# Loading the keys of one head pair and the values of the pair before it as one row of 56,832 B per partition, in a two-layer decode step

## The chip, the cores and the metric

The kernel runs on one core of one Trainium2 chip. The metric is the device time of one execution in microseconds (us); the time before is the median of three runs, 517.92 us (517.42 to 518.12).

## The reference, cut to what matters

One token (`Sq = 1`, width 640) passes twice through the same attention layer and the same MLP, with the same weights and the same cache both times. There are 32 heads of width 192, each with its own keys and values, and attention sees the last 4,096 positions.

```python
W = min(4096, max(256, Sk // 4))
q = (x @ wq)                                  # 640 -> 32 heads x 192
scores = einsum("bhqd,bhkd->bhqk", q, k) * Dh ** -0.5
o = einsum("bhqk,bhkd->bhqd", softmax(scores), v)
attention = o @ wo
mlp = (sigmoid(x @ w_gate) * (x @ w_up)) @ w_down
x = x + attention(layernorm(x)); x = x + mlp(layernorm(x))      # twice
```

## The kernel before, in words

**Units.** The 32 heads are handled as 16 pairs (`NPAIR`). A pair has two units of 14,208 bf16 values, 28,416 B, in each of the 128 partitions. The unit "a" holds the query weights of the pair and its keys; it lies in DRAM as `ua[p]`. The unit "b" holds its values (12,288 elements, `VE`) and its rows of the output weights (1,920 elements, `WOE`); it lies as `ub[p]`. One DMA loads one unit: 128 rows, one for each partition.

**Places.** One SBUF tensor, `big`, holds seven slots of one unit each and a region of 12,288 elements behind them (line 120), in which the MLP's weights and, in layer 1, the values of pair 1 (`PM`) are put. `big` is laid at a 256 B boundary, after the tensors `cst` and `sh`; `cst` is allocated first, at the default alignment of 32 B. `A_SLOT` and `B_SLOT` (lines 184 to 190) say which slot a unit goes to: in layer 0 the keys alternate between slots 0 and 1, the values between 2 and 3. Pairs 0, 14 and 15 stay in SBUF for layer 1 (`KEPT`), as does the key unit of pair 1, so that layer 1 begins with them while the stream goes on.

**Order of the loads.** `seq` (lines 195 to 209) is the one list of loads, issued in that order by SP: keys 0, keys 1, values 0, output weights of pair 0 into slot 2 (`wo0`), keys 2, values 1, and so on; the last values of each layer come in parts (`b1`, `b0`); then the MLP's weights, and for layer 1 the same from pair 2 to pair 13. `prefetch` (line 288) issues the next load as soon as the program, written down in the order of the compute, has released its slot (`release`): a key unit after the scores of its pair (QK, line 369), a value unit after the product with the output weights (PVn, line 454). On the chip SP waits at each load for a semaphore that says so. Each slot has one semaphore for its loads (`s0` to `s6`), and each user of a slot waits for that slot's load.

**One step** (lines 467 to 478) of pair p: PVn of pair p-2 (in layer 0), the query (Q, line 351), the scores (QK, line 366), the maximum over them (lines 376 to 385) by DVE, ACT and a matmul (line 382), the exponential (line 390), the product of values p-1 (PVmm, line 420), the transposition of the exponentials (ET, line 396), the normalized output of pair p-1 (PVt, line 436), and in layer 1 PVn of pair p-1 (line 450). PE takes its instructions in this order. The steps of pairs 2 to 15 in layer 0 and 4 to 13 in layer 1 are loops on PE; a loop needs the same addresses in each second step, which is why the output weights of pair 0 are in slot 2 in layer 0, and POOL copies them to slot 5, behind the values of pair 0, for layer 1 (line 460).

**The end.** After the last values come the gate, up and down weights of the last MLP (`fg`, `fu`, `fd`); between the loops and the last product (line 634), GpSimd (POOL) clears the semaphores and all engines meet (lines 759 and 760).

Of the kernel before, what the change touches and what calls it, by code (L numbers as in the profile page):

```python
# [13 lines left out]
P = 128  # L14
# [91 lines left out]
def decode_kernel(ctx: ExitStack, nc, cx: bass.AP, ua: bass.AP, ub: bass.AP,  # L106
# [10 lines left out]

    cst = sb("cst", [P, CE + CE % 2], BF16)
    sh = sb("sh", [P, 6 * DC + 8 + FC], BF16, 4)
    big = sb("big", [P, NSLOT * UNIT + ME], BF16, 256)  # L120
    M0 = NSLOT * UNIT
# [5 lines left out]
    sc = sb("sc", [P, 24 + 5 * DC + 2 * FC], FP32)  # L127
# [7 lines left out]
    ones_f = ones_c.to_broadcast([P, P])  # L135
    xq = sh[:, 0:DC]
# [29 lines left out]
    rslot = [res(f"slot{i}") for i in range(NSLOT)]  # L166
    rc = [res(f"cell{i}") for i in range(-(-ME // FW))]
# [4 lines left out]

    def slot(s, o, n):
        return big[:, s * UNIT + o:s * UNIT + o + n]
# [9 lines left out]
    A_SLOT = [{p: p % 2 for p in range(NPAIR)}, {p: 5 if p % 2 else 2 for p in range(NPAIR)}]  # L184
    B_SLOT = [{p: 2 + p % 2 for p in range(NPAIR)}, {p: 3 if p % 2 else 6 for p in range(NPAIR)}]
# [9 lines left out]
    def stream(l, ps):  # L195
        q = list(ps)
        out_ = []
        for i, p in enumerate(q):
            out_.append(("a", l, p))
            if i:  # L200
                out_.append(("b", l, q[i - 1]))
        return out_ + [("b1", l, q[-1]), ("b0", l, q[-1], 0), ("b0", l, q[-1], 1)]
    seq = stream(0, range(NPAIR))
    seq.insert(seq.index(("b", 0, 0)) + 1, ("wo0",))
    seq += [("wol", 14), ("wol", 15)] + [(k,) for k in (*MW, *MV)]
    tail = stream(1, range(2, 14))
    assert tail[0] == ("a", 1, 2)
    seq += [("wom",), ("a0", 0), ("a0", 1)] + tail[1:]
    seq += [("fg",), ("fu",), ("fd", 0), ("fd", 1), ("fd", 2)]
    seq_pos = [0]  # L210
    busy = {2}
# [12 lines left out]

    def try_load(it):
        k = it[0]
        if k in ("a", "b"):
            s = (A_SLOT if k == "a" else B_SLOT)[it[1]][it[2]]
            if not take(s):
                return False  # L230
            n, n0 = VE if it in (("b", 0, 0), ("b", 0, 14)) else UNIT, len(pg.ops["dma"])
            pg.dma(q_dma(slot(s, 0, n), (ua if k == "a" else ub)[it[2]][:, 0:n]), f"s{s}", wr=[rslot[s]])
            if it == ("b", 0, 14):
                ev_done["b14"] = list(pg.ops["dma"][n0]["deps"].items())
        elif k == "b1":
            s = B_SLOT[it[1]][it[2]]
            if not take(s):
                return False
            n, o1 = len(pg.ops["dma"]), UNIT if it[1] else VE
            pg.dma(q_dma(slot(s, NB * DH, o1 - NB * DH), ub[it[2]][:, NB * DH:o1]), f"s{s}", wr=[rslot[s]])  # L240
            ev_done["b1"] = list(pg.ops["dma"][n]["deps"].items())
        elif k == "b0":
            s = B_SLOT[it[1]][it[2]]
            o = it[3] * NHALF
            pg.dma(q_dma(slot(s, o, NHALF), ub[it[2]][:, o:o + NHALF]), f"bh{it[3]}", wr=[res(f"bh{it[3]}")], extra=ev_done["b1"])
        elif k == "a0":
            if f"a14_{it[1]}" not in ev_done:
                return False
            s = A_SLOT[1][2]
            o0, o1 = ((0, A0CUT), (A0CUT, UNIT))[it[1]]  # L250
            pg.dma(q_dma(slot(s, o0, o1 - o0), ua[2][:, o0:o1]), f"a0{it[1]}", wr=[res(f"a0{it[1]}")] + ([rslot[s]] if it[1] else []),
                   extra=[ev_done[f"a14_{it[1]}"]])
        elif k == "wo0":
            s = B_SLOT[0][2]
            pg.dma(q_dma(slot(s, VE, WOE), ub[0][:, VE:UNIT]), f"s{s}", wr=[rslot[s]])
        elif k == "wol":
            s = B_SLOT[0][it[1]]
            pg.dma(q_dma(slot(s, VE, WOE), ub[it[1]][:, VE:UNIT]), f"wol{it[1]}", wr=[res(f"wol{it[1]}")], extra=ev_done["b1" if it[1] == 15 else "b14"])
        elif k in MW:
            if any(n not in ev_done for n in MAFTER.get(k, ())):  # L260
                return False
            c, f0, f1 = MW[k]
            src = {"w": wg_d, "u": wu_d, "d": wd_d}[k[0]]
            pg.dma(q_dma(mreg(c * FW, (f1 - f0) * FW), src[:, f0 * FW:f1 * FW]), k, wr=rc[c:c + f1 - f0])
        elif k in MV:
            if VAFTER[k] not in ev_done:
                return False
            c0, c1 = MV[k]
            o0, o1 = c0 * FW, min(c1 * FW, ME)
            pg.dma(q_dma(mreg(o0, o1 - o0), ub[PM][:, o0:o1]), k, wr=rc[c0:c1])  # L270
        elif k == "wom":
            if "QM" not in ev_done:
                return False
            pg.dma(q_dma(slot(A_SLOT[1][PM], 0, WOE), ub[PM][:, VE:UNIT]), "wom", wr=[res("wom")], extra=[ev_done["QM"]])
        elif k == "fg":
            pg.dma(q_dma(mreg(0, 12 * FW), wg_d), "fg", wr=rc)
        elif k == "fu":
            if not take(U_SLOT):
                return False
            pg.dma(q_dma(slot(U_SLOT, 0, 12 * FW), wu_d), f"s{U_SLOT}", wr=[rslot[U_SLOT]])  # L280
        else:
            if it[1] == 0 and not take(D_SLOT):
                return False
            c0, c1 = WFIN[it[1]]
            pg.dma(q_dma(slot(D_SLOT, c0 * D, (c1 - c0) * D), wdp(c0, c1)), f"wf{it[1]}", wr=[rslot[D_SLOT]] if it[1] == 0 else [])
        return True
# [13 lines left out]
    pg.dma(q_dma(cst[:, 0:CE], cx), "x", wr=[res("cst")], q="adma")  # L300
    prefetch()
# [35 lines left out]
    def attention(l, xi):  # L337
# [70 lines left out]
        def PVmm(p, z):  # L408
# [3 lines left out]
            for h in (1, 0) if half else (0, 1):  # L412
                vt = (mreg(h * NB * DH, NB * DH) if inm else slot(sv, h * NB * DH, NB * DH)).rearrange("p (t d) -> p t d", t=NB)
                for part in (0, 1) if half and h == 0 else (None,):
                    us = range(NB // 2) if part is None else range(part * NB // 4, (part + 1) * NB // 4)

                    def f(t, h=h, vt=vt, us=us):
                        for u in us:
                            j = u % 4
                            ins = t.matmul(o8[h][32 * j:32 * j + 2, 0:2 * DH].rearrange("p (a d) -> p a d", a=2), lhsT=et_sb[:, z, h * NB + 2 * u:h * NB + 2 * u + 2],  # L420
                                           rhs=vt[:, 2 * u:2 * u + 2, :], start=(u < 4), stop=(u >= NB // 2 - 4), tile_position=(0, 32 * j))
                        return ins
                    rV = rc if inm else [rslot[sv]] + ([] if part is None else [res(f"bh{part}")])
                    pg.op("pe", f, rd=[res(f"et{z}")] + rV, ex=[rb[4 + h]])
                pg.op("act", lambda a, h=h: a.copy(out=o8_sb[:, :, h * DH:(h + 1) * DH], in_=o8[h][:, 0:2 * DH].rearrange("p (a d) -> p a d", a=2)),  # L425
                      wr=[res(f"o8sb{h}")], ex=[rb[4 + h]])
# [15 lines left out]
        def PVn(p, z):  # L442
            inm = l == 1 and p == PM
            sv = None if inm else 2 if l == 0 and p == 0 else B_SLOT[l][p]
            wo = slot(A_SLOT[1][PM], 0, WOE) if inm else slot(sv, VE, WOE)
# [8 lines left out]
            pg.op("pe", im, rd=[res(f"oTb{z}")] + ([res("wom"), rslot[sa]] if inm else [rslot[sv]]) + ([res(f"wol{p}")] if p > 13 or (l == 1 and p == 0) else []), ex=[rb[7]])  # L454
            if inm:
                release(sa)
            elif not (l == 0 and ("b", p) in KEPT):
                release(sv)
            if l == 0 and p == 0:
                pg.op("pool", lambda g: g.tensor_copy(out=slot(5, VE, WOE), in_=slot(2, VE, WOE)), rd=[rslot[2]], wr=[res("wol0")])  # L460
                release(2)
# [302 lines left out]
def _layout(inputs):  # L764
# [6 lines left out]
    ua = np.empty((NPAIR, P, UNIT), bf)  # L771
    ub = np.empty((NPAIR, P, UNIT), bf)
    q = wq.reshape(DC, P, NPAIR, 2, DH)
    qv = ua[:, :, :WQE].reshape(NPAIR, P, DC, 2 * DH)
    for h in range(2):
        qv[..., h * P:(h + 1) * P] = q[:, :, :, h, :P].transpose(2, 1, 0, 3)
        qv[..., 2 * P + h * 64:2 * P + (h + 1) * 64] = q[:, :, :, h, P:].transpose(2, 1, 0, 3)
        ua[:, :, WQE + h * W:WQE + (h + 1) * W] = k[:, h, :, :P].transpose(0, 2, 1)
        ua[:, h * 64:(h + 1) * 64, WQE + 2 * W:] = k[:, h, :, P:].transpose(0, 2, 1)
    ua[:, :, :WQE] = qv.reshape(NPAIR, P, WQE)  # L780
    ub[:, :, :VE] = v.transpose(0, 5, 1, 2, 4, 3, 6).reshape(NPAIR, P, VE)
    ub[:, :, VE:] = wo.reshape(NPAIR, P, WOE)
# [19 lines left out]
    return dict(cx=cx, ua=ua, ub=ub, wg=blk(wg), wu=blk(wu), wd=wdn)  # L802
# [17 lines left out]
```

## Time and profile before

| | |
|---|---|
| median of three runs | 517.92 us |
| the profiled execution's own time | 518.12 us |
| its span | 516.8 us |
| PE, DVE, ACT, POOL busy | 275.3, 97.9, 87.7, 2.0 us |
| moved by DMA | 219.45 MB, 11,835 packets |
| transfers of 3,552 KB (one unit): keys, values | 27, 24 |
| from issue to landing, median: keys, values | 29.8, 28.2 us |
| mean granted TensorE clock | 0.598 |

The span is the time from the first to the last instruction or packet; the run's time has 1.3 us more around it. Busy times are shares of engines that work at the same time, so they do not add up. The time from issue to landing has in it the time that a transfer stands in the queue behind earlier ones. In the timeline, times are us from the span's start; the column after the start is the length, and what stands in brackets is how long the engine had been idle and what ended that.

### The profile page before, as it was taken

The numbers are of one execution on the slowest core, as the hardware profiler recorded it, in microseconds if no ns is written. First come the engines' busy times: TensorE is split into PE (matmuls) and PEld (weight loads), VectorE is DVE, ScalarE is ACT, GpSimd is POOL, SyncE is SP. The second block draws the span as 40 slices with busy tenths as digits, with TensorE's granted clock in tenths as the row PEclk, the third lists the DMA queues.
The fourth block names the chain that finished last, engine by engine and source line by source line (L and its number), as shares of the span: only waits on it lengthen the run. The fifth ranks groups of instructions, "written<-read, shape, count | busy, mean of one in ns | idle before, by whom it ended". The sixth has DMA issues, their size and how long they took to land.

```text
span 516.8 us, 8422 instructions
## 1 busy us (share of the span) xinstructions
PE 275.3 (53%) x3716; PEld 139.7 (27%) x3716; DVE 97.9 (19%) x372; ACT 87.7 (17%) x171; POOL 2.0 (0%) x5
## 2 busy tenths in 40 slices
PE   0645454544545453635465667777554545455465
PEld 0322122212222222212224434433222212222234
DVE  1222111211121201111121233232211211121211
ACT  0112102210121112210120023123202211121120
POOL 0010000000000000000000000000000000000000
PEclk9987566556555555565565568666566555555555
DMA  8999999999999999999999999999999999999996
GB/s 357 430 436 432 427 435 433 427 435 440 427 433 438 431 427 438 433 429 431 433 417 411 392 440 428 430 437 432 430 433 432 427 435 433 431 436 435 423 427 282
DMA packets 11835, 219.45 MB, mean 425 GB/s; under 512 B 1448, under 2 KB 1448, under 8 KB 4264
## 3 DMA queue, kind: packets, MB, share of 16 engines
q1 hardware_dynamic: 11672, 219.13, 99.1%
q8 instruction: 13, 0.21, 0.1%
q10 hardware_dynamic: 144, 0.06, 0.0%
q14 instruction: 6, 0.05, 0.0%
HBM read 219.18 MB, written 0.00 MB: 424 GB/s over the span
## 4 chain that ended last, share of the span: by engine, by line
DMA 73%; PE 18%; DVE 4%; SPq 2%; issue 1%; ACT 1%; ACTq 0%; DVEq 0%
DMA big<-in_ub_dram 61%; PE o L420 8%; DMA big<-in_wd_dram 7%; DMA big<-in_wu_dram 4%; PE scores L366 3%; PE bank L403 2%; SPq L182 2%; PE bank L450 1%; PE bank L396 1%; ACT e_sb L390 1%; DVE sc L405 1%; PE bank L382 1%; DVE et_sb L400 1%; DVE sh L439 1%; PE bank L351 1%
## 5 line engine op out<-in xcount | busy, mean ns | idle before, releaser
L420 PE MATMUL o<-big,et_sb 128*2 128x384 bf16 x1024 | 85.7, 508 | 50.1 <-DMA big<-in_ub_dram 50.0
L366 PE MATMUL scores<-big,qs 128*32 128x512 bf16 x744 | 83.0, 614 | 9.9 <-DVE qs L354 9.8
L379 ACT ACTIVATE diag<-cst,sc 128x128 f32<-128x128 bf16 x32 | 12.9, 402 | 262.5 <-DVE sc L376 247.7
L351 PE MATMUL bank<-sh,big 128*128 128x1 bf16 x480 | 17.6, 166 | 69.3 <-DMA big<-in_ua_dram 68.3
L420 PEld LDWEIGHTS o<-big,et_sb 128*2 128x2 bf16 x1024 | 29.0, 113 | 93.7 <-DMA big<-in_ub_dram 58.9
L376 DVE TENSOR_REDUCE sc<-scores 128x1 f32<-128x1024 f32 x31 | 37.9, 1224 | 80.9 <-PE scores L366 80.9
L382 PE MATMUL bank<-diag,sc 128*128 128x128 f32 x64 | 23.1, 458 | 47.4 <-ACT diag L379 47.4
L390 ACT ACTIVATE e_sb<-scores,sc 128x1024 bf16<-128x1024 f32 x31 | 37.3, 1204 | 41.5 <-DVE sc L385 39.7
L425 ACT CAST o_sb<-o 128x384 bf16<-128x384 f32 x64 | 30.4, 476 | 71.3 <-PE o L420 71.2
L366 PEld LDWEIGHTS scores<-big,qs 128*32 128x32 bf16 x744 | 23.7, 132 | 44.3 <-issue 31.1
L351 PEld LDWEIGHTS bank<-sh,big 128*128 128x128 bf16 x480 | 15.8, 106 | 72.2 <-DMA big<-in_ua_dram 70.1
L382 PEld LDWEIGHTS bank<-diag,sc 128*128 128x128 f32 x64 | 14.5, 282 | 72.6 <-ACT diag L379 70.8
L400 DVE CAST et_sb<-bank 128x64 bf16<-128x64 f32 x32 | 7.2, 224 | 122.9 <-PE bank L396 122.9
L354 DVE TENSOR_TENSOR qs<-bank,cst 128x96 bf16<-128x96 f32 x32 | 8.2, 258 | 100.5 <-PE bank L351 100.3
L450 PE MATMUL bank<-sh,big 128*128 128x1 bf16 x480 | 17.4, 165 | 15.5 <-DVE sh L439 15.3
L403 PE MATMUL bank<-sc 128*128 128x2 f32 x64 | 16.0, 319 | 14.5 <-DVE sc L401 14.5
L450 PEld LDWEIGHTS bank<-sh,big 128*128 128x128 bf16 x480 | 14.8, 101 | 18.0 <-DVE sh L439 17.3
L403 PEld LDWEIGHTS bank<-sc 128*128 128x128 f32 x64 | 13.2, 257 | 17.3 <-DVE sc L401 17.3
L383 DVE TENSOR_REDUCE sc<-bank 128x2 f32<-128x128 f32 x32 | 9.3, 292 | 42.5 <-PE bank L382 42.5
L396 PEld LDWEIGHTS bank<-cst,e_sb 128*128 128x128 bf16 x256 | 9.2, 104 | 23.3 <-ACT o_sb L425 16.8
L396 PE MATMUL bank<-cst,e_sb 128*128 128x8 bf16 x256 | 11.9, 170 | 5.7 <-ACT e_sb L390 5.7
L405 DVE RECIPROCAL sc<-bank 64x1 f32<-64x1 f32 x64 | 10.6, 166 | 20.0 <-PE bank L403 18.9
(61 smaller groups left out, 100.6 us busy)
## 6 DMA issues: line engine op xcount, KB each, us to landing
big<-in_ua_dram SPq DMA_DIRECT2D x27, 3552.0 KB, 29.8
big<-in_ub_dram SPq DMA_DIRECT2D x24, 3552.0 KB, 28.2
big<-in_ub_dram SPq DMA_DIRECT2D x2, 3072.0 KB, 26.6
big<-in_ub_dram SPq DMA_DIRECT2D x4, 768.0 KB, 17.2
big<-in_wd_dram SPq DMA_DIRECT2D x3, 960.0 KB, 7.1
big<-in_ua_dram SPq DMA_DIRECT2D x1, 2048.0 KB, 12.2
big<-in_ub_dram SPq DMA_DIRECT2D x1, 2016.0 KB, 16.2
big<-in_ub_dram SPq DMA_DIRECT2D x4, 480.0 KB, 17.8
```

What stands on the lines that cost most here:

```text
L351: ins = t.matmul(qe[:, i:i + 1], lhsT=slot(sa, c * 2 * DH + c0, P), rhs=xq[:, c:c + 1], start=(c == 0), stop=(c == DC - 1))
L366: ins = t.matmul(sc_x[1 + b][32 * j:32 * j + 32, :], lhsT=qs[:, y, k, :], rhs=slot(sa, WQE + k * W + (4 * b + j) * 512, 512), start=(k == ...
L376: pg.op("dve", lambda v: v.reduce_max(out=mx, in_=sc_x[0][:], axis=AX.X), wr=[res("mx")], ex=sc_x[3:5])
L379: pg.op("act", lambda a: a.mul(out=diag[:], in_=ident, mul=mx), rd=[res("cst"), res("mx")], wr=[res("diag")])
L382: pg.op("pe", lambda t: t.matmul(dmx[:, 0:P], lhsT=ones_f, rhs=diag[:], start=True, stop=True), rd=[res("diag"), res("ones")], ex=[rb[2]])
L390: pg.op("act", lambda a: a.activation(out=e_sb[:], in_=sc_x[0][:], func=ACT.Exp, bias=nbias, scale=srs_c, accum_out=rowsum), rd=[res("nbia ...
L396: ins = t.matmul(qe[:, 0:2 * NB].rearrange("p (r x) -> p r x", r=2)[:, :, 4 * b:4 * b + 4], lhsT=e_sb[:, b * P:(b + 1) * P], rhs=sel, star ...
L403: pg.op("pe", lambda t: t.matmul(dmx[:, P:P + 2], lhsT=ones_f, rhs=rs2, start=True, stop=True), rd=[res("rs2"), res("ones")], ex=[rb[2]])
L405: pg.op("dve", lambda v, h=h: v.reciprocal(out=Rn[z][64 * h:64 * h + 64], in_=dmx[64 * h:64 * h + 64, P + h:P + h + 1]), wr=[res(f"Rn{z}{h ...
L420: ins = t.matmul(o8[h][32 * j:32 * j + 2, 0:2 * DH].rearrange("p (a d) -> p a d", a=2), lhsT=et_sb[:, z, h * NB + 2 * u:h * NB + 2 * u + 2 ...
L425: pg.op("act", lambda a, h=h: a.copy(out=o8_sb[:, :, h * DH:(h + 1) * DH], in_=o8[h][:, 0:2 * DH].rearrange("p (a d) -> p a d", a=2)), wr= ...
L450: ins = t.matmul(yT[:, j:j + 1], lhsT=wo[:, c * D + j * P:c * D + (j + 1) * P], rhs=oTb[z][:, c:c + 1], start=False, stop=(c == 2), skip_g ...
```

## The change

- Keys of pair p and values of pair p-1 stand side by side in DRAM, as the row `uc[p]` of two units, 56,832 B in each partition, and go to two neighbouring slots. A new map `PLACE` puts slot 3 beside slot 0 and slot 2 beside slot 1. One DMA, kind "c", loads both. Which of the two comes first alternates with p; within a value unit the output weights stand ahead of the values for even pairs, behind them for odd pairs (`v_at`, `wo_at`).
- In layer 0, c1 to c14 take the place of keys 1 to 14 and values 0 to 13, and the list starts with keys 0 and c1. Keys 15 and values 14 and 15 are still loaded alone. In layer 1, c4 to c12 take the place of keys 4 to 12 and values 3 to 11; keys 2, 3 and 13 and values 2, 12 and 13 are loaded alone.
- A c is issued when both its slots are released. Its semaphore (`c00`, `c01`, `c10`, `c11`: layer, parity of p) serves both units.
- The products that read values or output weights wait for POOL instead of for the DMA: `values_in` sets one element (`tick`) to 0 on POOL when the load has landed, once for each c and for three values loaded alone (`b`).
- The separate load `wo0` is gone. The output weights of pair 0 come with c1 into slot 5, and POOL copies them from there to slot 2 ahead of the first step.
- `big` is allocated first and no longer at a 256 B boundary; `cst` follows it, and `sh` comes last, both at 32 B.

```diff
-    sh = sb("sh", [P, 6 * DC + 8 + FC], BF16, 4)
-    big = sb("big", [P, NSLOT * UNIT + ME], BF16, 256)
+    big = sb("big", [P, NSLOT * UNIT + ME], BF16)
...
+    PLACE = {s: i for i, s in enumerate((0, 3, 2, 1, 4, 5, 6))}
+
     def slot(s, o, n):
-        return big[:, s * UNIT + o:s * UNIT + o + n]
+        return big[:, PLACE[s] * UNIT + o:PLACE[s] * UNIT + o + n]
...
-    A_SLOT = [{p: p % 2 for p in range(NPAIR)}, {p: 5 if p % 2 else 2 for p in range(NPAIR)}]
-    B_SLOT = [{p: 2 + p % 2 for p in range(NPAIR)}, {p: 3 if p % 2 else 6 for p in range(NPAIR)}]
+    A_SLOT = [{p: p % 2 for p in range(NPAIR)}, {p: 6 if p % 2 else 3 for p in range(NPAIR)}]
+    B_SLOT = [{p: 2 + p % 2 for p in range(NPAIR)}, {p: 2 if p % 2 else 5 for p in range(NPAIR)}]
...
+    seq = [("a", 0, 0)] + [("c", 0, p) for p in range(1, 15)] + [("a", 0, 15), ("b", 0, 14)] + last_values(0, 15)
+    seq += [("wol", 14), ("wol", 15)] + [(k,) for k in (*MW, *MV)] + [("wom",), ("a0", 0), ("a0", 1), ("a", 1, 3), ("b", 1, 2)]
+    seq += [("c", 1, p) for p in range(4, 13)] + [("a", 1, 13), ("b", 1, 12)] + last_values(1, 13)
...
+    def values_in(s):
+        pg.op("pool", lambda g: g.memset(tick, 0.0), rd=[rslot[s], res("tick")], wr=[rval[s], res("tick")])
...
+        if k == "c":
+            l, p = it[1:]
+            ss = A_SLOT[l][p], B_SLOT[l][p - 1]
+            if any(x in busy for x in ss):
+                return False
+            busy.update(ss)
+            first = min(ss, key=PLACE.get)
+            pg.dma(q_dma(slot(first, 0, 2 * UNIT), uc[p]), f"c{l}{p % 2}", wr=[rslot[x] for x in ss])
+            values_in(ss[1])
...
-            pg.dma(q_dma(slot(s, VE, WOE), ub[0][:, VE:UNIT]), f"s{s}", wr=[rslot[s]])
...
+    pg.op("pool", lambda g: g.tensor_copy(out=slot(2, wo_at(0), WOE), in_=slot(5, wo_at(0), WOE)), rd=[rslot[5]], wr=[rslot[2]])
...
-                pg.op("pool", lambda g: g.tensor_copy(out=slot(5, VE, WOE), in_=slot(2, VE, WOE)), rd=[rslot[2]], wr=[res("wol0")])
```

## The prediction

> **What bounds the kernel now.** I read the page's slices first, then the chain of waits in order of time, then the timeline of single steps.
>
> ```profile
> span 516.8 us, 8422 instructions
> ...
> PE 275.3 (53%) x3716; PEld 139.7 (27%) x3716; DVE 97.9 (19%) x372; ACT 87.7 (17%) x171; POOL 2.0 (0%) x5
> ...
> DMA  8999999999999999999999999999999999999996
> ...
> DMA packets 11835, 219.45 MB, mean 425 GB/s; under 512 B 1448, under 2 KB 1448, under 8 KB 4264
> ```
>
> The 16 DMA engines are busy in every slice while no compute engine reaches 54%. The stream of keys, values and weights is the bound, and a change counts only through the time that the DMA engines need, or through a gap in their queue.
>
> ```profile
> 408.01 2.73 PE o L420 x32
> ...
> 413.15 28.41 DMA big<-in_ub_dram
> 441.61 2.73 PE o L420 x32
> ```
>
> From one value product (L420) to the one two pairs later the chain takes 441.61 - 408.01 = 33.60 us; four transfers of 128 rows x 28,416 B pass in it, so one takes 8.40 us.
>
> The trace keeps start, duration and size of each DMA packet. A row is one packet, eight rows of a transfer go through each engine, and a 4-byte semaphore packet closes them. On one engine the next packet starts 1,049.4 ns after a 28,416 B packet, 908.3 after a 24,576 B one, 146 after a 3,840 B one, and 6 ns after a semaphore packet. The line through the outer two is (1,049.4 - 146) / 24,576 = 0.03676 ns per byte, plus **4.8 ns per packet** whatever its size (24,576 B: 903.4 + 4.8 = 908.2, as seen). A transfer is 8 x 1,049.4 + 6 = 8,401 ns; all but 44.4 ns of it is bytes.
>
> **What is saved.** Layer 0 has c1 to c14 in place of fourteen key and fourteen value transfers, and the separate first output weights (wo0) go too: 15 transfers fewer. Layer 1 has c4 to c12: 9 fewer. Bytes are the same. Each removed transfer takes 8 packets and one semaphore from each engine: 24 x (8 x 4.8 + 6) = 24 x 44.4 = **1.07 us**, if a 56,832 B row goes as one packet on the same line. It follows from that line, not from a packet of such a size, of which the trace has none. Bounds: 24 x 6 = 0.14 us if rows are cut in two again; at most 1.07 from this source, since nothing else is saved. I take 1.07, as all fourteen sizes from 2,560 to 28,416 B lie on the line within 1 ns.
> The Trainium skill ("DMA: Bandwidth & Descriptors", Why small descriptors are slow) gives about 3 cycles per packet; at its 850 MHz that is an estimate of 3.5 ns against the 4.8 measured, and would make the saving 0.82 us.
>
> **Where big lies.** The constants come first (the trace's first POOL rows write four of them), each at a multiple of 32 B, so big, now allocated next and at 32, starts at byte 160 of each partition, off the 256 B boundary. Before, all large rows start on one. The nearest row is cst: before, it lies first and at 32, thus at that same byte 160, and its 482 B source rows start anywhere. While its packets alternate with the first transfer's, that transfer's spacing is 1,072.8 ns: 23.4 ns for a cst packet, against 482 x 0.03676 + 4.8 = 22.5 on the line. So being off a boundary cost at most 0.9 ns per packet. Changed, each engine moves 81 - 24 = 57 such transfers of 8 packets, 456: at most 0.41 us if it is per packet. If those 0.9 ns were per 256 B piece, of which a cst row touches at least two, 0.45 ns x 53,500 pieces (219.13 MB / 16 / 256) would be 24 us. Nothing below zero: a boundary lost cannot help. I take 0, since 482 B rounded up to 32 B pieces (512 x 0.03676 + 4.8 = 23.6) explains all of the 23.4.
> A rule speaks against the change: the same page (How a descriptor splits into AXI transactions) says that a descriptor off a 256 B boundary starts from the boundary below and pays for the unused beats. At byte 160 that is 5 beats; an estimate by its 850 MHz is 5.9 ns per packet, 2.7 us over 456, a net loss of 1.6 us. The cst packets show no such 5.9 ns.
>
> **What is coarser.** A c can be issued only when both its slots have been read: the keys by QK, the values by PVn. How long is that after landing? The first step in which all data was there:
>
> ```profile
> 22.98 0.54 PE L351 MATMUL bank<-sh,big 128*128 128x1 bf16 x15
> ...
> 28.45 0.80 PE L382 MATMUL bank<-diag,sc 128*128 128x128 f32 x2 [1.82 <-ACT diag L379]
> ...
> 29.17 2.73 PE L420 MATMUL o<-big,et_sb 128*2 128x384 bf16 x32
> ...
> 33.76 0.53 PE L450 MATMUL bank<-sh,big 128*128 128x1 bf16 x15 [0.56 <-DVE sh L439]
> 34.39 0.33 SPq L182 DMA_DIRECT2D big<-in_ub_dram  x1
> ```
>
> From Q (L351) to the end of PVn (L450) are 34.29 - 22.98 = 11.3 us; SP issues 0.1 later. The first issue of the program (0.75) had its first packet at 2.13, so 1.4 us more: 12.8 in all. The next c lands 16.7 us after the one being used, and the engines of one transfer finish 2.3 to 2.5 us apart, so the earliest is free after 14.2. Margin 1.4 us for it, 3.9 for the latest, which alone sets the end. No gap. At the start, c1 lands at about 29.7 (its semaphore covers a1 too, so Q(1) is 7 us later than now); PVn(0) ends at 41.0 and c3 follows, before c2's earliest engine ends (44.9). Free.
>
> The turn to layer 1 is tightest, since PE is behind there:
>
> ```profile
> 347.41 0.33 SPq L182 DMA_DIRECT2D big<-in_ua_dram  x1
> 355.07 0.33 SPq L182 DMA_DIRECT2D big<-in_ub_dram  x1
> ```
>
> c4 waits for PVn(15) (319.1) and c5 for PVn(PM) (331.8); the data ahead ends at 323.8 and 340.8. c6 (keys 6, values 5) waits for what releases the second line, 355.07, not for the first. c5's last engine ends at 357.6, and c6's first packet is due at 356.4: 1.2 us to spare. Cost 0; were PE 1 us later, still 0.
>
> At the end of layer 0, Q(15) must now follow step 14, which starts at c14's landing (248.8): 260.1 in place of 257.26, the product of values 14 at 266.1 in place of 264.49. Behind it lie waits that swallow the 1.6 us:
>
> ```profile
> 271.88 0.81 PE L420 MATMUL o<-big,et_sb 128*2 128x384 bf16 x8 [1.03 <-DMA big<-in_ub_dram]
> ...
> 276.54 0.96 PE L573 MATMUL scores<-sh,big 128*128 128x1 bf16 x30 [0.95 <-DMA big<-in_wg_dram]
> ```
>
> All data and step 14 with it come 15 x 44.4 ns = 0.67 us earlier, so PE reaches the first row 1.6 - 0.67 = 0.9 us later than now and starts it 0.1 earlier (1.03 - 0.9); the first gate (second row), its data 0.67 earlier, still waits 0.95 - 0.67 + 0.1 = 0.4. DMA still leads. At the end of layer 1 the product of values 12 comes at 491.4, its data at 491.0, and part two of the last value product still waits 1.03 us before (500.51). Hidden.
>
> **POOL.** 26 memsets of one element stand between a value's landing and PE: 0.10 us each by the constants' rows, on an engine with 2.0 us of work in 516.8. The value product comes 5.9 us after its landing, which hides them; for values 14 and 12, which come alone, 0.1 to 0.3 us lies within the waits just named. The copy of wo0 (1.78 us, L460) now runs at c1's landing, 9 us ahead of its reader. Five more semaphores are cleared before the last product; between the last DVE row (511.69) and that product (512.63) lie 0.94 us for some 30, so at most 0.16 us, and the final weights land after it anyway (514.3).
>
> **The sum.** 518.12 (profiled time; span 516.8 and 1.3 around it) - 1.07 = 517.05. The median lies 0.20 below the profiled run: **516.85**.
>
> **Rivals.**
> 1. The saving isn't there: rows are cut in two, 0.14 us, **517.8**. For it: no packet over 28,416 B in the trace. Against: none of the rows there is was cut.
> 2. Slower, by the lost boundary: a packet pays from byte 160. It decides from 1.07 us / 456 = 2.3 ns per packet on; if the boundary makes of each packet two, at 4.8 ns, it is 2.2 us and **519.0**; at 0.45 ns per 256 B 541. For: all large rows of before lie on a boundary, so none shows the price. Against: cst, at most 0.9 ns.
> 3. The queue runs dry: two slots hang on one release. It costs nothing until a step takes over 15.3 us from landing to PVn (16.7 - 1.4), then every excess microsecond some 20 times; at 15.4, 2 us: **518.9**. At the turn it starts with 1.2 us, once. Against: later steps add up to 11.3 us too (240.41 to 246.33 from Q to the value product's turn, 248.86 to 254.21 from there to PVn's end).
> 4. More than the sum: the last engine of a transfer, late by 2.5 us through instruction fetches on it, catches up. Up to 1 us, **516**.
>
> **Chances.** Forecast 0.58 (516.4 to 517.3), rival 1 0.08, rival 2 0.15, rival 3 0.12, rival 4 0.07. About 0.2% (1.04 us) is what a measurement of this kernel can tell from no change, and the forecast sits on that line: 0.36 of it beyond, 0.22 within. Faster 0.36 + 0.07 = 0.43; same 0.22 + 0.08 + 0.05 (small cases of 2 and 3) = 0.35; slower 0.13 + 0.09 = 0.22. The range 516.2 to 519.2 leaves out 0.16: the ends of 2, 3 and 4.
>
> **What would show it.** 57 transfers into big in place of 81, packets of 56,832 B, 2,094 ns apart (0.03676 x 56,832 + 4.8). 2,100 or more condemns the boundary. A transfer c every 16.76 us; c6 issued before c5's last packet; DMA slices still full between 320 and 360. The forecast fails if packets stay at 28,416 B, if spacing grows by over 4 ns, or if the queue shows gaps before a c.

## The result, and the profile after

The changed kernel takes **520.92 us** in the median of 6 runs (520.21 to 521.53), the kernel before 517.97 beside it (6 runs, 517.32 to 518.18). The ratio is 1.0059, 95% interval 1.0046 to 1.0072: slower by 3 us, where 1.1 us less than before was forecast. The profiled execution of the changed kernel took 520.21 us, its span 518.8.

The page of the changed kernel, in the lines that answer to those shown of before:

```profile
span 518.8 us, 8457 instructions
...
PE 264.1 (51%) x3716; PEld 136.1 (26%) x3716; DVE 97.8 (19%) x372; ACT 84.9 (16%) x171; POOL 4.3 (1%) x31
...
DMA  8999999999999999999999999999999999999996
GB/s 355 473 435 421 413 430 425 438 453 421 429 434 421 456 429 434 425 429 432 421 410 397 391 437 466 426 422 378 457 425 429 439 421 425 429 451 408 425 424 284
DMA packets 8380, 219.46 MB, mean 423 GB/s; under 512 B 1064, under 2 KB 1064, under 8 KB 3752
...
big<-in_uc_dram SPq DMA_DIRECT2D x23, 7104.0 KB, 22.3
```

The change did what it says: 23 transfers of 7,104 KB, 8,380 packets in place of 11,835, the same bytes. The DMA engines still look full in every slice, but in tenths: a slice is 13 us, and 0.5 us of idling does not show there. The line of GB/s is finer. Its 28th slice (350 to 363 us) holds 378, and in the kernel before no slice between 300 and 500 us is below 420. (408 in the 37th is no gap: bytes count in the slice in which a packet starts, and rows are now twice as wide.)

The chain of waits of the changed kernel at that place, then one step on (start, length, what):

```profile
354.81 0.57 PE bank L483 x15
355.45 20.82 DMA big<-in_uc_dram
376.32 0.58 PE bank L382 x15
...
387.26 0.58 PE bank L483 x15
387.90 21.79 DMA big<-in_uc_dram
```

L382 is Q, L483 the output product PVn (L351 and L450 before); SP issues at L200. PVn(3), which starts at 354.81, releases the second slot of c6, and SP issues c6 at 355.45. On the first DMA engine, the one that finishes first, c5 ended at 355.47. So its queue was empty: from there it took 18.68 us to the end of c6 (374.15), where the line of the prediction gives 16.76. The last three rows show the usual step: Q at 376.32, PVn over at 387.84, **11.5 us** from landing to release.

From the packets of the two traces, the ends of matching transfers on the first and on the last DMA engine. All packet times in this document are the packets' own plus 0.37 us, by about which the update of a semaphore follows its packet in these traces; so is the 2.13 of the prediction. The leads in the expectations of e13, e15 and e18 are without it.

```
                                     before             changed
values 13 / c14 (layer 0)            246.56 / 248.84    246.68 / 248.24
first-layer weights                  286.59 / 288.78    286.83 / 289.05
values 4 / c5 (layer 1)              355.09 / 357.63    355.47 / 358.54
values 5 / c6                        371.89 / 374.43    374.15 / 375.54
values 11 / c12                      472.70 / 475.24    475.16 / 476.76
last weights                         512.74 / 514.30    514.70 / 516.15
```

The saving of 15 x 44.4 ns should have put c14 0.7 us ahead. Its first engine is 0.1 behind, its last 0.6 ahead, the mean of the sixteen 0.06 ahead. From c5 to c6 the first engine loses 1.9 us, the mean 1.1, the last 0.2; from there to the end the mean loses another 0.3. Two losses, then: one spread over the transfers, and one at a place. A third, 0.4 us of the mean, lies between the first-layer weights and values 2 of layer 1, where no c is loaded; it stays open.

The spread one is in the packets. Over the line of the prediction (0.03676 ns per byte + 4.8), the mean of what a packet takes more, in ns, packets that are late by over 100 left out:

```
row, bytes                     6,144   15,360   24,576   28,416   56,832
before, big at byte 768         -0.1      0.0      0.0      0.2       -
changed, big at byte 160         3.0      4.1      4.0      2.4      2.7
```

The trace does not name a packet's engine; packets are joined by their times, which makes the means good to about half a ns. The bytes at which `big` starts follow from the order of allocation; no view shows them. Before, nearly every packet lies on the line. Changed, about half of the 56,832 B packets are within 1 ns of it (2,094 ns apart, as predicted); most others lie up to 12 ns above it. Whole transfers go one way or the other: c5, c7 and c8 of layer 0 end 16.76 us after the transfer ahead on most engines, as the line has it, c9 and c11 to c14 16.79 us after it, 4 ns per packet more on all engines alike. Why some pay nothing stays open.

### The profile page after: what moved, and what is told of

The parts are those of the page before. It is cut to its first block, busy times and chain, and to the rows that moved or that the text cites. A ratio compares the mean times of both kernels' runs of the same rounds, so it can differ in the third digit from the quotient of the medians.

```text
span 518.8 us, 8457 instructions
## 1 busy us (share of the span) xinstructions
PE 264.1 (51%) x3716; PEld 136.1 (26%) x3716; DVE 97.8 (19%) x372; ACT 84.9 (16%) x171; POOL 4.3 (1%) x31
## 2 busy tenths in 40 slices
DMA packets 8380, 219.46 MB, mean 423 GB/s; under 512 B 1064, under 2 KB 1064, under 8 KB 3752
## 4 chain that ended last, share of the span: by engine, by line
DMA 61%; PE 25%; DVE 8%; ACT 3%; issue 2%; SPq 1%; ACTq 0%; DVEq 0%
DMA big<-in_uc_dram 51%; PE scores L397 9%; PE o L451 7%; DMA big<-in_wd_dram 6%; DVE sc L407 4%; DMA big<-in_wu_dram 3%; PE bank L413 2%; PE bank L434 2%; PE bank L382 2%; ACT e_sb L421 2%; PE bank L483 2%; SPq L200 1%; ACT diag L410 1%; PE bank L427 1%; DVE sc L436 1%
## 5 line engine op out<-in xcount | busy, mean ns | idle before, releaser
L397 PE MATMUL scores<-big,qs 128*32 128x512 bf16 x744 | 84.4, 623 | 9.9 <-DVE qs L385 9.8
L382 PE MATMUL bank<-sh,big 128*128 128x1 bf16 x480 | 17.6, 166 | 126.6 <-DMA big<-in_uc_dram 125.7
L451 PE MATMUL o<-big,et_sb 128*2 128x384 bf16 x1024 | 78.0, 472 | 2.0 <-DMA big<-in_uc_dram 2.0
L382 PEld LDWEIGHTS bank<-sh,big 128*128 128x128 bf16 x480 | 15.4, 105 | 129.5 <-DMA big<-in_uc_dram 127.6
L451 PEld LDWEIGHTS o<-big,et_sb 128*2 128x2 bf16 x1024 | 27.7, 108 | 39.0 <-issue 31.4
L483 PE MATMUL bank<-sh,big 128*128 128x1 bf16 x480 | 17.2, 165 | 16.5 <-DVE sh L472 16.1
L434 PE MATMUL bank<-sc 128*128 128x2 f32 x64 | 14.1, 290 | 14.5 <-DVE sc L432 14.5
L483 PEld LDWEIGHTS bank<-sh,big 128*128 128x128 bf16 x480 | 14.6, 99 | 19.0 <-DVE sh L472 13.1
L434 PEld LDWEIGHTS bank<-sc 128*128 128x128 f32 x64 | 11.3, 222 | 17.3 <-DVE sc L432 17.3
L427 PE MATMUL bank<-cst,e_sb 128*128 128x8 bf16 x256 | 11.6, 169 | 8.3 <-ACT e_sb L421 8.3
```

The costliest lines, as they stand in the source:

```text
L382: ins = t.matmul(qe[:, i:i + 1], lhsT=slot(sa, c * 2 * DH + c0, P), rhs=xq[:, c:c + 1], start=(c == 0), stop=(c == DC - 1))
L397: ins = t.matmul(sc_x[1 + b][32 * j:32 * j + 32, :], lhsT=qs[:, y, k, :], rhs=slot(sa, WQE + k * W + (4 * b + j) * 512, 512), start=(k == ...
L427: ins = t.matmul(qe[:, 0:2 * NB].rearrange("p (r x) -> p r x", r=2)[:, :, 4 * b:4 * b + 4], lhsT=e_sb[:, b * P:(b + 1) * P], rhs=sel, star ...
L434: pg.op("pe", lambda t: t.matmul(dmx[:, P:P + 2], lhsT=ones_f, rhs=rs2, start=True, stop=True), rd=[res("rs2"), res("ones")], ex=[rb[2]])
L483: ins = t.matmul(yT[:, j:j + 1], lhsT=wo[:, c * D + j * P:c * D + (j + 1) * P], rhs=oTb[z][:, c:c + 1], start=False, stop=(c == 2), skip_g ...
```

## The experiments

Each ratio is to runs of the kernel before on the same chip (medians of before: 517.8 to 518.2), with its 95% interval.

**1. The boundary alone, taken out of the change.** `e1_aligned` is the changed kernel with the allocation of before:

```diff
+    cst = sb("cst", ...)
+    sh = sb("sh", [P, 6 * DC + 8 + FC], BF16, 4)
+    big = sb("big", [P, NSLOT * UNIT + ME], BF16, 256)
```

> The changed kernel with big laid back at a 256 B boundary, allocated as before; nothing else. Theory A (the lost boundary costs 2 to 4 ns per packet of any size, 456 packets): 1.2 to 1.8 us less than the changed kernel's 520.92, about 519.4, and every 56,832 B packet exactly 2,094 ns apart as most are now. Theory B (the queue runs dry at c4 and c6, two slots on one release): the time stays within 0.3 us of 520.9, and the late first packets at 61.6 and 356.8 us stay. Theory C (a row of 56,832 B is itself uneven): spacing stays uneven as it is now. A and B can both hold; then it is 519.4 with the late first packets still there.

Measured: 519.61 (9 runs), ratio 1.0034 [1.0020, 1.0048], against 1.0059 of the changed kernel: 1.3 us (by the intervals 0.3 to 2.3). Nearly all packets are back on the line. The gap at c6 stays:

```profile
GB/s 357 440 463 431 419 432 424 431 462 427 427 431 427 427 462 431 427 431 427 424 411 409 389 440 461 419 441 380 437 449 435 423 440 422 431 453 408 422 430 289
```

The 28th slice has 380. So the boundary is one cause and not the only one. The profiled execution, at 518.10, is the fastest of the nine: what makes the median 1.5 us longer is not in this trace.

**2. The boundary alone, put into before.** `e2_before_off` is the kernel before with `big` allocated first, at byte 160. `e8_before_192` and `e9_before_1152` put it at bytes 192 (a multiple of 64) and 1,152 (a multiple of 128).

> The kernel before with big at byte 160, allocated first and at 32 B as in the change; nothing else. Theory A: 648 packets of each engine at 2 to 4 ns are 1.3 to 2.6 us, about 519.9, and packets of every size spread by up to 12 ns. Theories B and C: 517.97, no spread.

> The kernel before with big at byte 192 of each partition, off a 256 B boundary but on one of 64 B. If only a 256 B boundary helps: 520.6, as at byte 160. If 64 B are enough: 518.0.

> The kernel before with big at byte 1,152, on a boundary of 128 B and off one of 256 B. If only a 256 B boundary helps: 520.6. If 64 or 128 B are enough: 518.0.

Measured: 520.62, 520.76 and 520.68; ratios 1.0048 [1.0035, 1.0061], 1.0054 [1.0040, 1.0069], 1.0048 [1.0033, 1.0062]. In all three, 28,416 B packets lie about 4 ns over the line in the mean (3.9 to 4.3). 648 packets of big per engine x 4 ns = 2.6 us; measured are 2.5 to 2.8. Byte 768 costs nothing; 64 and 128 B boundaries are as bad as 32. With three positions alike, the boundary of 256 B is shown as a cause by itself. (Byte 768 is the only start on one that was measured.)

**3. The release of two slots at once.** `e4_two_halves` keeps the joint release but loads each c as two transfers of 128 rows x 28,416 B, back to back. `e5_layer1_single` loads the pairs of layer 1 singly, each released alone. Both have `big` on the 256 B boundary again (`aligned`).

```diff
-            pg.dma(q_dma(slot(first, 0, 2 * UNIT), uc[p]), f"c{l}{p % 2}", ...)
+            ev = pg.dma(q_dma(slot(first, 0, UNIT), uc[p][:, 0:UNIT]), f"c{l}{p % 2}", ...)
+            rslot[second].w = pg.dma(q_dma(slot(second, 0, UNIT), uc[p][:, UNIT:2 * UNIT]), f"h{l}{p % 2}")
```

```diff
-    seq += [("c", 1, p) for p in range(4, 13)] + [("a", 1, 13), ("b", 1, 12)] + ...
+    for p in range(4, 14):
+        seq += [("a", 1, p), ("b", 1, p - 1)]
```

> As e1_aligned, but each c is two DMAs of 28,416 B rows, issued one right behind the other once both slots are released; the scores wait for both as they wait for one c. It has the coarse release without the wide rows. Theory B: the late first packets stay, so it is e1_aligned plus the 23 x 44.4 ns of the transfers that come back, 1.0 us more. Theory C: it is even with the kernel before but for the late packets, and faster than e1_aligned.

> As e1_aligned, but layer 1 loads keys 4 to 12 and values 3 to 11 one by one as before the change, each issued when its own slot is free; layer 0 keeps its c. Theory B: the late first packets at 356.8 us are gone; their 1.0 us or so is saved and 9 x 44.4 ns = 0.4 us is given back: 0.6 us less than e1_aligned. Theory A alone: 0.4 us more than e1_aligned.

Measured: e4 520.49, ratio 1.0033 [1.0014, 1.0053], with dips in its GB/s in the slices around 318 and 357 us (404 and 347); e5 518.35, ratio 1.0007 [0.9996, 1.0018], with no dip there:

```profile
GB/s 358 450 456 433 421 424 433 424 429 463 433 428 424 438 424 428 463 433 428 410 413 420 407 444 425 434 432 438 423 435 429 441 428 430 435 436 435 421 433 287
```

Without joint release in layer 1 the kernel is 0.0027 faster than e1, 1.4 us, though it gives up 9 x 44.4 ns = 0.4 us of the saving: the joint release costs some 1.8 us there (the intervals allow 0.9 to 2.7). The traces show the place: from c5 to c6 the mean of the sixteen engines loses 1.1 us against the kernel before in the changed kernel, 1.0 in e1, 2.7 in e4 and nothing in e5. e5's profiled execution, at 516.35, is the fastest of its eleven. e4 beside e1 shows no gain from wide rows; its runs spread over 4.5 us.

**4. All of the change but the wide transfers.** `e6_all_single`: `big` on the boundary, no c at all; POOL's memsets, the new rows in DRAM, the new places and the early copy of wo0 stay.

> The changed kernel with big at a 256 B boundary and no c at all: keys and values are loaded one by one from the new rows, the memsets on POOL, the new places of the slots and the early copy of the first output weights stay. Theory B (what is left after the boundary is the coarse release): the time of the kernel before within 0.3 us, since the output weights of pair 0 no longer cost a transfer and the rest is hidden. Rival D (the POOL hop or the new order of rows costs): over 518.5.

Measured: 518.16, ratio 1.0011 [1.0003, 1.0020]. The rest costs 0.5 us (0.2 to 1.0); the prediction had it hidden. In its profiled execution (517.90, the fastest of its twelve) the last load ends 0.27 us earlier than in before, so the trace does not show where; this stays open.

**5. Release early.** If the joint release is what hurts, take the value product of the pair ahead first, then Q and QK, and PVn in the middle of the step. `e7_early_release`:

```diff
 def step(p, prev):
-    if l == 0 and prev > 0:
-        PVn(prev - 1, 1 - prev % 2)
+    PVmm(prev, prev % 2)
     Q(p, 0)
     QK(p, 0)
+    PVt(prev % 2)
+    if prev < 14:
+        PVn(prev, prev % 2)
     soft()
     expo()
-    PVmm(prev, prev % 2)
     ET(p % 2)
-    PVt(prev % 2)
-    if l == 1:
-        PVn(prev, prev % 2)
```

> As e1_aligned (all c, boundary kept), but in each step of the loops PE takes the product of values and both products with the weights before the softmax chain, so that both slots of a c are free some 5 us earlier; the last two steps of layer 0 are written out. Theory B: no late first packets, and the 24 transfers less are a gain at last: 516.9, 1.1 us under the kernel before, with a small spread. Rival D, or rows of 56,832 B being slow as such: it stays at the 519.6 of e1_aligned.

Measured: **525.17**, ratio 1.0135 [1.0113, 1.0157], far off. The timeline of its PE and SP says why (start, length, then the idle time before and what ended it):

```profile
257.45 25.79 SPq L200 DMA_DIRECT2D big<-in_wu_dram  x3
...
263.65 2.73 PE L451 MATMUL o<-big,et_sb 128*2 128x384 bf16 x32 [4.67 <-POOL sc L235]
266.32 0.56 PE L382 MATMUL bank<-sh,big 128*128 128x1 bf16 x15
```

The last step of a layer is different: values 14 come alone, after keys 15. Keys 15 had landed at 256, but Q(15) (L382) now stood behind the value product, which waited for 263.5. The chain from there ran 6.6 us later than in e1 up to the product that frees the place of the third up-weight transfer; SP issued that at 282.9, when the transfer ahead of it had ended at 279.0 to 280.5. One step of my own making, not the early release itself.

`e10_early_fixed` writes out the last two steps of each layer's loop, the very last in the old order.

```diff
+    if p == (15, 13)[l]:
+        Q(p, 0)
+        QK(p, 0)
+        soft()
+        expo()
+        PVmm(prev, prev % 2)
...
+            loop(1, 12)
+            step(14, 13)
+            step(15, 14)
...
+            loop(3, 8)
+            step(12, 11)
+            step(13, 12)
```

> Aligned version of the change (big at byte 768) with the early release of e7, but the last step of each layer (keys 15 with values 14, keys 13 with values 12, whose values come alone and after the keys) in the old order. In e7 these steps put the value product ahead of Q on PE, so Q(15) waited for a landing at 263.5 in place of 256; the up weights were issued 6.6 us late and the DMA queue stood empty for 6 us. Theory (the lost boundary and the coarse release are all that the change costs beyond its saving): every c is dispatched over 5 us before the previous c's first engine ends, no gap at c4 or c6, 517.8 - 1.07 = 516.7, ratio 0.998; with the 0.4 us that the version with single loads showed beyond before, 517.1. Rival (the wide rows cost time by themselves, or the early order costs PE as much as it gives): 518.2 or more, ratio 1.001 or more.

> e10 again, one profiled execution, since the first (517.83) lay below the median of its other runs (518.53). If that difference is a matter of the turn to layer 1, its packets from the weights of layer 0 on come later than in the first; if it is packets that are slower everywhere, the spacing of 56,832 B packets is not 2,094 ns.

Measured: 518.53 (11 runs), ratio 1.0014 [1.0004, 1.0025]: 1 us better than e1, but not the 516.7 of the theory. The profiled executions took 517.83 and 518.07. A step of it in the chain of waits:

```profile
80.54 0.10 POOL sc L235
...
80.69 2.73 PE o L451 x32
...
86.30 0.54 PE bank L483 x15
...
86.91 27.02 DMA big<-in_uc_dram
```

From POOL's memset at landing (80.54) to the next issue (86.91) are 6.4 us in place of 11.6. From c5 to c6 the mean of the engines now loses nothing. One c still came late in both profiles: c4 of layer 1, issued 1.7 and 2.5 us before the first engine had finished the transfer ahead; there the last engine loses 1.2 and 1.3 us. In the first profile the first engine ends the last load 0.85 us before that of the kernel before (511.89 against 512.74), the last engine only 0.28 (514.02 against 514.30).

**6. The boundary and the wide rows once more, with the early release.** `e12_early_off` is e10 with the allocation of the change; `e11_early_halves` is e10 with the halves of e4.

> e10 with the order of allocation of the change, so big at byte 160: the boundary alone, without thin leads. Boundary theory: 2.3 to 3.9 ns mean excess per packet, 456 packets of big per engine and some 500 in all: 1.1 to 1.9 us over e10. Rival (the loss of the changed kernel against its aligned version came from the thin leads, not from the packets): within 0.4 us of e10.

> e10, but each c as two transfers of 128 rows x 28,416 B issued back to back, so that only the width of the rows and the number of transfers differ. Packet line of the prediction: 24 transfers more x 44.4 ns = 1.07 us over e10, 517.8 if e10 gives 516.7. Rival (a row of 56,832 B saves nothing that can be seen): within 0.3 us of e10.

Measured: e12 520.59, ratio 1.0054 [1.0040, 1.0068], 2.1 us above e10 (1.2 to 3.0); 56,832 B packets 3.6 ns over the line in the mean. e11 518.89, ratio 1.0021 [1.0009, 1.0034], 0.4 us above e10, which its interval does not tell from 0 or from 1.07.

**7. The turn to layer 1.** `e13_turn_single` is e10 with keys 4 and values 3 of layer 1 loaded singly; `e14_turn_halves` the same with halves.

> e10 with keys 4 and values 3 of layer 1 as two single transfers (its step in the old order). In e10 only one transfer still came late: c4, dispatched 1.3 us before the first and 3.2 us before the last engine of the transfer ahead had ended; the gap of the last engine over the first grew there from 1.9 to 3.0 us. Theory (a lead below about 3.4 us is what the coarse release costs, the packet line holds): no first packet late by over 0.1 us on several engines after the weights, first engine of the last load at 511.9, last one about 1 us earlier than in e10, median 0.5 to 1 us below e10 in the same call's terms: ratio 0.998 to 1.000. Rival (something that shows in no packet of e10, as its median lies 0.7 us above its profiled execution): as e10, 1.001 or more.

> e13 with each c as two transfers of 128 rows x 28,416 B, so that the width of the rows is all that differs, without any late first packet. Packet line: 22 transfers more x 44.4 ns = 0.98 us above e13. Rival (wide rows save nothing): within 0.3 us of e13.

Measured: e13 519.56, ratio 1.0030 [1.0015, 1.0046]; e14 520.77, 1.0062 [1.0049, 1.0075]. The expectation of e13 fell. Its trace has nothing late at keys 4, but a late c6, issued 2.1 us before c5's first engine was done: the place moved by two pairs, since PE was still behind. What it shows there is small (four engines late, the mean loses 0.03 us), so it does not account for the 1 us that e13 lies above e10. `e15_c_from_7` loads all of keys 4 to 6 and values 3 to 5 singly, `e16_c7_halves` adds the halves.

> Aligned, early release in layer 0 and from step 7 of layer 1 on, and the whole catch-up after the turn (keys 4 to 6, values 3 to 5 of layer 1) as single transfers in the old order, so that wide transfers c stand only where they are dispatched over 4 us ahead: c1 to c14 and c7 to c12, 21 transfers fewer than before. e13 had moved the late transfer from c4 to c6 (dispatched 1.7 us before the first engine of c5 ended); the theory that the turn is the rest of the loss gives 517.9 - 21 x 0.0444 = 517.0, ratio 0.998, and a spread of its runs as small as that of the kernel before. Rival (something else is left, in the early order or the wide rows): 518.2 or more, ratio 1.001 or more.

> e15 with each c as two transfers of 128 rows x 28,416 B: packet line 21 x 44.4 ns = 0.93 us above e15, so as before, 517.9. Rival (wide rows save nothing): within 0.3 us of e15.

Measured: e15 518.91, ratio 1.0020 [1.0008, 1.0031]; e16 519.13, 1.0026 [1.0013, 1.0039]. In e15 no transfer of layer 1 has late first packets on more than one engine, and its first engine is done at 511.97, 0.8 us before that of before. But the last engine is done at 514.62, 0.3 later than there. Steps that are written out make more code to fetch. The page's line of the queue that fetches instructions is

```profile
q8 instruction: 13, 0.21, 0.2%
```

in the changed kernel (13 in the one before, too), and in e15

```profile
q8 instruction: 18, 0.29, 0.2%
```

Each such fetch is one packet of 16,384 B that sits for about 0.9 us on one DMA engine, between the packets of the stream; an engine that is hit falls back and does not catch up while the queue is full. In e15 the gap between first and last engine grows from 2.4 to 3.8 us during the transfer that ends at 421.5, when a fetch was recorded (415.5), and is still 3.8 at 488.6. The users of a transfer wait for its last engine: in the changed kernel the landings of c6 run from 374.18 to 376.27, and Q starts at 376.32. Over all traces, the last load ends with a gap of 0.95 to 1.84 us in the twelve with 13 or 14 fetches and of 1.99 to 2.65 us in the eight with 16 or 18.

**8. Few fetches, wide rows in layer 0 alone.** `e17_layer0_only`: e10's order in layer 0, e5's single loads in layer 1, 14 fetches. `e18_layer0_late`: e5 again beside it.

> Wide transfers in layer 0 alone (c1 to c14), aligned, with the early release there; layer 1 as in e5, all single and in the old order as one loop, so that only two steps are written out and the instruction fetches (13 in the kernel before, 16 to 18 in e10 to e16) are nearly those of before. Packet line: 15 x 44.4 ns = 0.67 us below 517.9, 517.2, ratio 0.9987. Theory (the extra fetches, which sit late in e10 and e15 and put one DMA engine 0.9 us behind each, were the rest of the loss): 517.2 to 517.6, and the last load's last engine at most 1.5 us behind its first. Rival (something else of the change costs a further 0.5 to 1 us): 518.2 or more.

> e5 once more, on the same chip as e17: it differs from e17 only in the step order of layer 0, where c is dispatched 3.1 to 4.5 us before the first engine of the c ahead has ended, in place of 6 to 8. If such a lead is too thin in some executions, its median lies 0.5 to 1.2 us above that of e17 and its runs spread wider; if 3.1 us is enough, the two are within 0.3 us.

Measured: e17 517.55, ratio 0.9995 [0.9983, 1.0008]; e18 517.96, ratio 0.9997 [0.9987, 1.0006]; before 518.16 (23 runs). The median of e17 is 0.6 us below before, as 15 x 44.4 ns = 0.67 have it, but the ratio makes it 0.3 and the interval holds no change as well. Between e17 and e18, a lead of 6.9 to 8.5 us in layer 0 in place of 3.4 to 4.8 brings at most some 0.9 us and perhaps nothing. No version beat the kernel before beyond doubt.

## Why the prediction was wrong

- **The lost boundary, taken at 0, is the first step that failed.** I bounded it at 0.9 ns per packet by the cst rows and chose 0. The packets show 2.4 to 4.1 ns in the mean (2.7 for the widest, whose sign of 2,100 ns was therefore not reached); rival 2 was to decide from 2.3 ns on, and it did. Price: 1.3 us (changed against e1), 2.1 (e12 against e10), 2.5 to 2.8 for the 648 packets of the kernel before. The bound came from one kind of packet of 482 B, a hundredth of a 56,832 B row, seen only between packets of another transfer; it did not carry over, and why is not shown. Nor is the price per 256 B piece: rows of 6,144 and 56,832 B pay about alike.
- The rule of the Trainium skill that I set aside spoke for the right sign ("DMA: Bandwidth & Descriptors", How a descriptor splits into AXI transactions: a start off 256 B fetches from the boundary below and pays for the unused beats). My estimate from it was 5.9 ns per packet at byte 160; measured are 2 to 4 on average and 0 to 12 on single ones. By its count of beats, byte 192 (six beats) should cost more than 160 and byte 1,152 (four) less; the runs show the three alike.
- **The joint release, "No gap", is the second.** The step itself was nearly right, 11.5 us for 11.3. Wrong was what follows the issue. I took 1.4 us to the first packet from the first issue of the program, when the queue was empty, and found 1.4 us to spare on top, a lead of 2.8 us. In the traces of all kernels with a c, count the engines on which the first packet of a 56,832 B row ended over 50 ns late: 27 of 27 that came free less than 2 us after the issue, 15 of 73 at 2.0 to 3.0 us, 26 of 86 at 3.1 to 3.6, 10 of 459 at 3.7 to 4.5, and 39 of 2,907 beyond. Of the 26, 12 belong to one transfer, c4 of layer 0 in the changed kernel, so this is no clean edge. Steady leads in the changed kernel are 3.0 to 4.8 us: partly too thin. That late c4, issued 3.1 us ahead, cost 0.5 us in the mean over the engines.
- **At the turn I had 1.2 us to spare and a cost of 0.** c6 was issued at 355.45 and c5's first engine ended at 355.47, where I had 355.07 and 357.6; 357.6 was the last engine. I compared the issue with that end alone, as the one "which alone sets the end". It is true that the last engine lost only 0.2 us at c6, but the first lost 1.9 and the mean 1.1, and at the end of the kernel first and last are both late, by 2.0 and 1.8. The joint release in layer 1 costs 1.8 us in the runs (e5 against e1, 0.9 to 2.7).
- **The packet line was right.** Rows of 56,832 B go as one packet 2,094 ns apart (rival 1 falls). The traces show the saving where the packets are on the line: at the end of c14, where the line gives 0.67 us, the mean over the engines is 0.58 to 0.72 us ahead of the kernel before in all nine traces of kernels with `big` on the boundary and whole rows in layer 0 (e1, e5, e7, e10 twice, e13, e15, e17, e18), and within 0.10 of it in the five with halves or single loads (e4, e6, e11, e14, e16). In the run times it is barely visible: halves cost 0.0007, 0.0032 and 0.0006 over the same kernel with whole rows (e11, e14, e16), 0.0015 in the mean, 0.8 us with some 0.5 to either side, for 0.93 to 1.07 by the line; e4 beside e1 gives -0.0001, give or take 0.0024.
- The end of layer 0, hidden: right, the first-layer weights arrive within 0.3 us of before. POOL, hidden: not settled, the rest of the change costs 0.5 us (e6) and no row shows where. Rival 4 (the last engine catches up) came in part: the gap at the end is 1.45 us, 1.56 before; it changes with every kernel. The gain of up to 1 us did not.
- The sum, by what was measured: -1.0 (line; -0.8 in runs) + 1.3 to 2.1 (boundary) + 1.8 (joint release in layer 1) + 0.5 (rest) = 2.6 to 3.4, for 3.0 measured. The sum is no closer than its terms, whose intervals are up to 1 us to either side. The runs of one kernel with a joint release lie up to 3.5 (e1) and 4.5 us (e4) apart, and that stays unexplained; that thin leads hang on PE's pace at the turn is argued from e13, not shown.

## What to carry to other kernels

In a kernel that lives from one full DMA queue, a merged transfer saves its packet overhead once, and pays with the release: it can be issued only when the last of its buffers is free, so count the lead from that release to the *first* DMA engine's end, and ask for what this kernel needed, about 4 us. Keep the destination of large rows on a 256 B boundary of SBUF, whatever else moves. And where a price is bounded by one kind of small packet, keep the rival's whole price in the range.

## What the runs showed that was not expected

- The price of a start off a 256 B boundary in SBUF is a scatter on single packets, from 0 to 12 ns over the line, which comes to about 4 ns in the mean of a transfer, at rows from 6 KB up and at bytes 160, 192 and 1,152 alike; some transfers of the changed kernel pay nothing. It hits the whole stream of a kernel through one line of allocation.
- From the issue of a transfer to its first packet the first, empty queue shows 1.4 us (1.0 by the packet's own time, 1.75); in a running stream, engines still found the data late 3.1 to 3.6 us after the issue in 26 of 86 cases.
- An instruction fetch is a 16,384 B packet that holds up one of the 16 DMA engines for about 0.9 us; with five more of them, from steps written out, the last engine of the last load ends 2.65 us behind the first (e15), 1.56 in the kernel before.
